# Two chunks of 256 tokens made one stretch of 512: input groups first, then four output tiles

## The chip, the cores and the metric

The kernel runs on one core of a Trainium2 chip. A core has five engines with queues of their own: TensorE (PE, with its weight loads as PEld), VectorE (DVE), ScalarE (ACT), GpSimd (POOL) and SyncE (SP, which here issues DMAs). Each runs its instructions in a fixed order and waits on semaphores. The metric is the time of one execution in device microseconds, as a median of runs.

## The reference

Linear attention with random features over 8 batches, 8 heads, 576 tokens and 64 dimensions, then a feed-forward layer over all 4608 tokens.

```
q_p, k_p = phi(q * scale), phi(k * scale)   # exp(x omega^T - |x|^2/2 - max) / sqrt(m), m = 128
kv  = einsum('bhsm,bhsd->bhmd', k_p, v);  z = sum(k_p, axis=2)
x   = (q_p kv) / (q_p z + 1e-6)             # heads joined: [4608, 512]
h   = x @ w_in                              # [4608, 2048]
out = (h * tanh(softplus(h))) @ w_out       # the function in between is "mish"
```

## The kernel before

**Number format.** A factor of a matmul is split into two f16 parts, a high one and a rest; a product is three matmuls (rest x high, high x rest, high x high). The high part is a cast on ACT (`cast`, L69) or DVE (L71), the rest a subtraction on DVE or POOL (`rest`, L78 and L80). The first tasks and chunk 0 are computed in f32 without the split.

**Attention** comes as 68 items in the order of the batches: a `k_task` for each batch and pair of heads (32), a `q_task` for each tile of 128 tokens (36). An item goes through stages: load; cast (`sk` or `sq`, ACT) and rest (POOL); feature matmuls (`pk` or `pq`, PE, L369); maximum and subtraction (DVE, L390 and L399); exp (ACT, L405); cast (`kp` or `qn`, ACT) and rest (DVE). A k item then has v's scaling (`vf`, ACT, L470, needs the scale `s_v` of the batch), its `pkv` matmuls (L482) and their cast. A q item has a transposing DMA (L517), its `pn` matmuls (L532), the division on DVE, the split into `xs` and a second transposing DMA into `xT` (L562), which the feed-forward layer reads.

**Feed-forward** goes by 18 chunks of 256 tokens. `ff_in(c)` makes 8 groups: each computes two blocks f of 128 hidden units for the chunk, 2 x 12 matmuls with 256 columns moving, into one bank of PSUM (`ph`, two buffers). ACT reads a bank with mish into `h` (L694), and after every two banks a split makes the high part of `g` (ACT, L69) and the rest (DVE, L80). Where a chunk holds tokens of two batches, whose scales differ, mish and split are done in two pieces (`spans`). `ff_out(c)` has two `po` tiles (one bank each) and adds up 16 blocks f with three matmuls of 512 columns each; `o_task` scales a finished tile on ACT and stores it.

**Order.** A clock of turns sets it: `step()` is one turn, in which each task on the agenda that is due runs a stage; what it yields is the number of turns to its next stage. From chunk 2 on, each pass of the loop calls `next` of `ff_in(c)`, a turn, `next` of `ff_out(c - 1)`, a turn: input groups of one chunk alternate with output matmuls of the chunk before, one group of 24 against 12. Items are given at the turns of FIRST (the first 18), and later when their count is under `pace`, which rises by about 4 in a chunk. From an item's start its cast comes 3 turns later, the feature matmuls 6, the exp 8; `pkv` 11; `pn` 12 (13 for q7). A late stage of an item is emitted ahead of the mish and split that the same turn holds, since it is older on the agenda. This order is what the program is built from; the scheduler of the framework then places each engine's instructions by priority and by when it expects them to be able to run. `behind_ff` keeps attention matmuls behind the last feed-forward matmul emitted.

**Start.** Chunk 0 and 1 have code of their own (`ff_in(0)`, `ff_in(1)`, `ff_out0`); the weights are split in between (`w_split`).

Of the kernel before, what the change touches and what calls it, by code (L numbers as in the profile page):

```python
# [30 lines left out]
def tile_kernel(  # L31
# [10 lines left out]
    nc = tc.nc  # L42
# [457 lines left out]
    xT = {}  # L500

    def q_task(nth, t):
        c, off = t * P // CH, t * P % CH
        if c not in xT:
            xT[c] = sb.tile([P, 2, KT, CH], F16, tag="xT", name=f"xT{c}", bufs=3)
        tiles = [[(4 * g + i) * P for i in range(4)] for g in range(2)]
        e = yield from features(qT[t], tiles, f"q{t}", nth, t < QF)
        if t < QF:
            yield from q_first(nth, t, e, off)
            return  # L510
        qn = sb.tile([P, 2, H, M], F16, tag="aq", name=f"qn{t}", bufs=QB)
        cast(by("kp", nth), qn[:, 0], e)
        yield 1
        rest(by("kplo", nth), qn[:, 1], e, qn[:, 0])
        yield 1
        qp = sb.tile([P, 2, H, P], F16, tag="ap", name=f"qp{t}", bufs=2)
        nc.sync.dma_start_transpose(  # L517
            out=qp.rearrange("p a h s -> p (a h) s"), in_=qn.rearrange("p a h m -> p (a h m)")
        )
        yield 2 if t > 9 else 3 if t > QF else 4  # L520
        x = sb.tile([P, H, D], F32, tag="x", name=f"x{t}", bufs=2)
        rd = sb.tile([P, H, 1], F32, tag="rd", name=f"rd{t}")
        pns = []
        with behind_ff():
            for g in range(2):
                pn = ps_a.tile([P, 4, D1], F32, tag="a", name=f"pn{t}_{g}", padded_shape=[P, 4, P])
                for i in range(4):
                    h = 4 * g + i
                    for b, lo, hi in spans(t * P, P):
                        must(HP, "kv", b)  # L530
                        for n, (a, y) in enumerate(((1, 0), (0, 1), (0, 0))):
                            nc.tensor.matmul(  # L532
                                out=pn[lo:hi, i, :], lhsT=qp[:, a, h, lo:hi], rhs=kv[b][:, h, y, :],
                                start=n == 0, stop=n == 2,
                            )
                pns.append(pn)
        yield 1
        for g, pn in enumerate(pns):
            hs = slice(4 * g, 4 * g + 4)

            k_den = TOP * TOP * TOP * KVC
            k_num = TOP * TOP * KVC
            dve.tensor_scalar(
                out=rd[:, hs], in0=pn[:, :, D:D1], scalar1=EPS * k_den, scalar2=k_num / k_den,
                op0=ALU.add, op1=ALU.mult,
            )
            dve.reciprocal(out=rd[:, hs], in_=rd[:, hs])
            xt = dve.tensor_tensor(
                out=x[:, hs, :], in0=pn[:, :, 0:D], in1=rd[:, hs].broadcast_to([P, 4, D]),
                op=ALU.mult,  # L550
            )
        anchors[30 + t] = (xt.ins,)
        yield from x_parts(nth, t, x)

    def x_parts(nth, t, x):
        c, off = t * P // CH, t * P % CH
        xs = sb.tile([P, 2, H * D], F16, tag="xs", name=f"xs{t}", bufs=2)
        xf = x.rearrange("p h d -> p (h d)")
        cast(act if nth < 20 else by("x", nth), xs[:, 0], xf)
        rest(by("xlo", nth), xs[:, 1], xf, xs[:, 0])  # L560
        yield 1
        nc.sync.dma_start_transpose(  # L562
            out=xT[c].rearrange("p a k s -> p (a k) s")[:, :, off:off + P],
            in_=xs.rearrange("p a c -> p (a c)"),
        )
        did("x", c)

    def q_first(nth, t, e, off):

        qp = sb.tile([P, H, P], F32, tag="ap", name=f"qp{t}", bufs=2)  # L570
        for g in range(2):
            hs = slice(4 * g, 4 * g + 4)
            pt = ps_a.tile([P, 4, P], F32, tag="a", name=f"pt{t}_{g}")
            for i in range(4):
                nc.tensor.transpose(out=pt[:, i, :], in_=e[:, 4 * g + i, :], identity=ident)
            cast(act, qp[:, hs, :], pt)
        yield 1
        x = sb.tile([P, H, D], F32, tag="x", name=f"x{t}", bufs=2)
        rd = sb.tile([P, H, 1], F32, tag="rd", name=f"rd{t}")
        for g in range(2):  # L580
            hs = slice(4 * g, 4 * g + 4)
            pn = ps_a.tile([P, 4, D1], F32, tag="a", name=f"pn{t}_{g}", padded_shape=[P, 4, P])
            for i in range(4):
                for b, lo, hi in spans(t * P, P):
                    must(HP, "kvf", b)
                    nc.tensor.matmul(
                        out=pn[lo:hi, i, :], lhsT=qp[:, 4 * g + i, lo:hi], rhs=kvf[b][:, 4 * g + i, :],
                        start=True, stop=True,
                    )
            dve.tensor_single_scalar(out=rd[:, hs], in_=pn[:, :, D:D1], scalar=EPS, op=ALU.add)  # L590
            dve.reciprocal(out=rd[:, hs], in_=rd[:, hs])
            if t * P < CH:
                xt = dve.tensor_tensor(
                    out=x[:, hs, :], in0=pn[:, :, 0:D], in1=rd[:, hs].broadcast_to([P, 4, D]),
                    op=ALU.mult,
                )
                continue
            for b, lo, hi in spans(t * P, P):
                xt = dve.scalar_tensor_tensor(
                    out=x[lo:hi, hs, :], in0=pn[lo:hi, :, 0:D], scalar=vstate[b][2][lo:hi],  # L600
                    in1=rd[lo:hi, hs].broadcast_to([hi - lo, 4, D]), op0=ALU.mult, op1=ALU.mult,
                )
        anchors[30 + t] = (xt.ins,)
        if t * P >= CH:
            yield from x_parts(nth, t, x)
            return
        yield 1
        px = ps_a.tile([P, KT, P], F32, tag="a", name=f"px{t}")
        for i in range(KT):
            nc.tensor.transpose(out=px[:, i, :], in_=x[:, 2 * i:2 * i + 2, :], identity=ident)  # L610
        anchors[40 + t] = (cast(act, xT0()[:, :, off:off + P], px).ins, xt.ins)
        if off == 0:
            spin(2, ident, x[:, 0:4, :].rearrange("p h d -> p (h d)"))
        did("x", 0)

    def xT0():
        return xT[0].rearrange("p a k s -> p (a k s)").bitcast(F32).rearrange("p (k s) -> p k s", k=KT)  # L620

    def g0(gr):
        return gT[0, gr].rearrange("p a f s -> p (a f s)").bitcast(F32).rearrange("p (f s) -> p f s", f=FG)
# [31 lines left out]

    def ff_in(c):

        must(2, "x", c)
        sp = [(b_scales(b) if c else None, lo, hi) for b, lo, hi in spans(c * CH, CH)]
        for gr in range(FT // FG):  # L660
            gT[c, gr] = sb.tile([P, 2, FG, CH], F16, tag="g", name=f"g{c}_{gr}", bufs=GB)
            for q in range(FG // FQ):
# [4 lines left out]
                for j in range(0, FQ, 2):  # L667
                    ph = ps_h.tile([P, 2, CH], F32, tag="h", name=f"ph{c}_{gr}_{q}_{j}")
                    for i in range(2):
# [4 lines left out]
                        for n, (a, y, k) in enumerate(mm):  # L674
                            ff_mm[0] = nc.tensor.matmul(  # L675
                                out=ph[:, i, :], lhsT=wi(a, k, f) if c else wi0(k, f),
                                rhs=xT[c][:, y, k, :] if c else xT0()[:, k, :],
                                start=n == 0, stop=n == len(mm) - 1,
                            )
                    if c == 0:  # L680
# [4 lines left out]
                    else:  # L685
                        later(1, mish, sp, h[:, j:j + 2, :], ph)
                        if j > 0:
                            later(2, g_split, c, gr, q, sp, h)
                    yield

    def mish(sp, h, ph):

# [9 lines left out]
    def g_split(c, gr, q, sp, h):  # L702
        sl = slice(q * FQ, (q + 1) * FQ)
        did("g", c, q)
        g = gT[c, gr]
        for us, lo, hi in sp:
            cast(by_c("g", c), g[:, 0, sl, lo:hi], h[:, :, lo:hi], us[:, 1:2])
            lo_ = rest(dve, g[:, 1, sl, lo:hi], h[:, :, lo:hi], g[:, 0, sl, lo:hi], us[:, 1:2])
        anchors["g"] = (lo_.ins, anchors["h"])

# [40 lines left out]
        nc.sync.dma_start(out=out[row:row + P, :], in_=o)  # L751


    GB, HB, QB = 4, 5, 1
    w_dma = nc.sync

    FIRST = (0, 1, 2, 3, 4, 4, 9, 9, 26, 28, 30, 32, 37, 40, 44, 58, 59, 68)
    WIS = (6, 7, 8, 9, 11, 12, 13, 14)
    W_MAX = (6, 5, 5, 4, 2, 2, 1, 1)
    WOS = (35, 34, 33, 32, 31, 30, 29, 28)  # L760
# [10 lines left out]
    GAP0 = {'load': 1, 'exp': 0, 'kv': 1}  # L771
    GAP = {'load': 3, 'hi': 1, 'lo': 2, 'exp': 1, 'kv': 2}

    ROLE = dict(hi="AA", lo="PP", kp="AA", kplo="DD", v="DD", vlo="PP", kv="AA", x="AD", xlo="PP", h="DD", h0="DD", gm="DD", g="DA", glo="PD")
    NE, CE = 9, 1
    ENG = {"A": act, "D": dve, "P": pool}

    def gap(what, name):
# [7 lines left out]

    def by(role, nth):
        return ENG[ROLE[role][nth >= NE]]

    def by_c(role, c):  # L790
        if c == 0 and role[0] == "h":
            return act
        return ENG[ROLE[role][c >= CE]]

    wmax = []
    for n in (0, 1):
# [94 lines left out]
    load_v(2, nc.sync)  # L891
    load_v(3, act)
    load_w(0)
    load_two("q", qT, 0, "xT", 3)
    for i in range(1, NB):
        load_w(i)
    start(v_task(0))
# [27 lines left out]
        step()  # L925
        step()
    next(fo, None)
    for c in range(2, NCH):
        fi, fo = ff_in(c), ff_out(c - 1)
        for j in range(8):  # L930
            if given[0] < min(pace(c + j / 8), len(items)):
                give()
            next(fi, None)
            step()
            next(fo, None)
            step()
        for gen in (fi, fo):
            next(gen, None)
    while agenda:
        step()  # L940
    for _ in ff_out(NCH - 1):
        step()
    while agenda:
        step()

# [40 lines left out]
```

## Time and profile before

| what | value |
|---|---|
| runs shown | 957.12, 955.04, 954.8 us; median 955.04 us |
| profiled execution | 957.28 us, its span 955.5 us |
| granted TensorE clock, mean | 0.995 |
| PE, ACT, DVE, POOL busy | 97%, 67%, 55%, 26% of the span |
| ph matmuls (L675) | 3392, of which 128 in f32 |
| po matmuls (L719) | 1632 |

The page gives busy time by engine, then slices of the span, DMA queues, the chain of work that ended last, and the costliest groups of instructions by line. In the timeline a row has start, length, engine, line, operation, names (out<-in), shapes and count, and in brackets how long the engine was idle before it and what ended that. In the chain a row has start, length and what was running. In the windows a row has the stretch, its length, busy time and count for PE, PEld, DVE, ACT and POOL, the granted clock, the busy share of the DMA engines and GB/s. A time of a helper's line (L69, L78, L80) belongs to many tiles; the names tell them apart. The mean duration of a matmul in a group (278 and 380 ns) is that of one matmul by itself; in a row of many they overlap, and the distance from start to start is less.

### The profile page before, as it was taken

The numbers are of one execution on the slowest core, as the hardware profiler recorded it, in microseconds if no ns is written. First come the engines' busy times: TensorE is split into PE (matmuls) and PEld (weight loads), VectorE is DVE, ScalarE is ACT, GpSimd is POOL, SyncE is SP. The second block draws the span as 40 slices with busy tenths as digits, with TensorE's granted clock in tenths as the row PEclk, the third lists the DMA queues.
The fourth block names the chain that finished last, engine by engine and source line by source line (L and its number), as shares of the span: only waits on it lengthen the run. The fifth ranks groups of instructions, "written<-read, shape, count | busy, mean of one in ns | idle before, by whom it ended". The sixth has DMA issues, their size and how long they took to land. (4 is left out here: it accounts for less than half of the span.)

```text
span 955.5 us, 19211 instructions
## 1 busy us (share of the span) xinstructions
PE 931.4 (97%) x8125; PEld 665.1 (70%) x8125; DVE 528.2 (55%) x930; ACT 641.1 (67%) x831; POOL 247.6 (26%) x153
## 2 busy tenths in 40 slices
PE   9899987999999999999999999999999999999998
PEld 6786753767777777777777776777777777666663
DVE  3879688584775476655665464654746555111110
ACT  5758885798787777777777675877857766332230
POOL 1313143252162125322433243321442130000000
PEclk9998999999999999999999999999999999999999
DMA  9954414432452247214432245302430233100000
GB/s 288 320 190 155 136 47 100 84 96 71 92 118 62 56 69 165 59 48 85 95 66 72 46 95 113 95 24 70 79 91 23 68 56 84 28 23 12 12 12 34
DMA packets 128214, 82.22 MB, mean 86 GB/s; under 512 B 106432, under 2 KB 106560, under 8 KB 128128
## 3 DMA queue, kind: packets, MB, share of 16 engines
q1 hardware_dynamic: 127392, 79.47, 33.4%
q10 hardware_dynamic: 736, 1.52, 0.6%
q8 instruction: 64, 1.05, 0.4%
q14 instruction: 22, 0.18, 0.1%
HBM read 46.37 MB, written 9.44 MB: 58 GB/s over the span
## 5 line engine op out<-in xcount | busy, mean ns | idle before, releaser
L675 PE MATMUL ph<-xT,w 128*128 128x256 f16 (+1 forms) x3392 | 411.2, 278 | 0.7 <-ACT xT L69 0.7
L719 PE MATMUL po<-wo,g 128*128 128x512 f16 x1632 | 374.3, 380 | 4.1 <-ACT wo L69 2.8
L675 PEld LDWEIGHTS <-w 128*128 128x128 f16 x3264 | 318.5, 98 | 61.8 <-issue 1.6
L719 PEld LDWEIGHTS <-g 128*128 128x128 f16 x1632 | 155.9, 98 | 168.1 <-issue 5.0
L694 ACT ACTIVATE h<-ph,us 128x512 f32<-128x512 f32 (+3 forms) x184 | 101.1, 574 | 201.2 <-PE ph L675 200.2
L80 DVE SCALAR_TENSOR_TENSOR g<-h,us,g 128x1024 f16<-128x1024 f32 (+3 forms) x92 | 104.6, 1150 | 132.2 <-ACT g L69 131.9
L78 POOL TENSOR_TENSOR sq<-fq,sq 64x1024 f16<-64x1024 f32 x31 | 74.4, 2401 | 225.7 <-ACT sq L69 125.0
L78 POOL TENSOR_TENSOR sk<-fk,sk 64x1152 f16<-64x1152 f32 x24 | 62.8, 2618 | 81.2 <-ACT sk L69 53.1
L69 ACT ACTIVATE g<-h,us 128x1024 f16<-128x1024 f32 (+3 forms) x92 | 82.4, 924 | 1.1
L78 POOL TENSOR_TENSOR xs<-x,xs 128x512 f16<-128x512 f32 x34 | 46.8, 1377 | 125.4 <-issue 69.1
L390 DVE TENSOR_REDUCE mxk<-pk 128x4 f32<-128x512 f32 (+1 forms) x96 | 49.6, 549 | 50.7 <-PE pk L369 37.1
L390 DVE TENSOR_REDUCE mxq<-pq 128x4 f32<-128x512 f32 x72 | 46.6, 682 | 51.1 <-PE pq L369 48.4
L694 ACT ACT_TABLE_LOAD x56 | 71.8, 1283 | 1.0
L405 ACT ACT_TABLE_LOAD x52 | 66.7, 1283 | 0.9
L78 DVE TENSOR_TENSOR qn<-eq,qn 128x1024 f16<-128x1024 f32 x31 | 39.4, 1270 | 46.1 <-ACT qn L69 46.1
L78 DVE TENSOR_TENSOR kp<-ek,kp 128x1152 f16<-128x1152 f32 x24 | 38.6, 1610 | 18.6 <-ACT kp L69 18.6
L69 ACT ACTIVATE o<-po,us 128x512 f32<-128x512 f32 (+1 forms) x38 | 25.9, 682 | 30.3 <-PE po L719 30.2
L405 ACT ACTIVATE eq<-eq,lnt 128x1024 f32<-128x1024 f32 x31 | 35.6, 1149 | 9.0 <-DVE eq L399 8.6
L78 POOL TENSOR_TENSOR vb<-vf,vb 128x640 f16<-128x640 f32 x24 | 35.7, 1496 | 19.5 <-DVE vb L71 17.9
L399 DVE TENSOR_TENSOR eq<-pq,mxq 128x512 f32<-128x512 f32 x62 | 39.8, 679 | 0.0
L399 DVE TENSOR_TENSOR ek<-pk,mxk 128x512 f32<-128x512 f32 (+1 forms) x72 | 37.5, 548 | 0.5
L369 PE MATMUL pq<-om,sq 128*128 128x128 f16 x496 | 32.8, 219 | 3.7 <-POOL sq L78 3.7
(119 smaller groups left out, 889.9 us busy)
## 6 DMA issues: line engine op xcount, KB each, us to landing
vf<-in_vL_dram SPq DMA_DIRECT2D x30, 325.0 KB, 3.5
out_dram<-o SPq DMA_DIRECT2D x36, 256.0 KB, 2.1
fq<-in_qT_dram SPq DMA_DIRECT2D x31, 256.0 KB, 3.4
fk<-in_kT_dram SPq DMA_DIRECT2D x24, 256.0 KB, 3.6
raw<-in_w_out_dram SPq DMA_DIRECT2D x5, 1024.0 KB, 6.8
wo<-in_w_in_dram SPq DMA_DIRECT2D x4, 1024.0 KB, 12.3
raw<-in_w_in_dram SPq DMA_DIRECT2D x4, 1024.0 KB, 14.9
wo<-in_w_out_dram SPq DMA_DIRECT2D x3, 1024.0 KB, 7.9
```

Of the source, the lines that this page charges most:

```text
L69: return act.activation(out, in_, AF.Copy, scale=scale)
L78: eng.tensor_tensor(out=out, in0=in_, in1=hi, op=ALU.subtract)
L80: return eng.scalar_tensor_tensor(out=out, in0=in_, scalar=scale, in1=hi, op0=ALU.mult, op1=ALU.subtract)
L369: nc.tensor.matmul(out=pp[:, i, :], lhsT=left[:, o:o + P], rhs=right, start=j == 0, stop=j == len(terms) - 1,)
L390: sub = dve.tensor_reduce(out=mx[:, lo:hi], in_=pp[:, :m, :], axis=AX.X, op=ALU.max, negate=by_act)
L399: sub = dve.tensor_tensor(out=e[:, lo:hi, :], in0=pp[:, :m, :], in1=mx[:, lo:hi].unsqueeze(2).broadcast_to([P, m, M]), op=ALU.subtract,)
L405: last = act.activation(e, e, AF.Exp, bias=lnt)
L675: ff_mm[0] = nc.tensor.matmul(out=ph[:, i, :], lhsT=wi(a, k, f) if c else wi0(k, f), rhs=xT[c][:, y, k, :] if c else xT0()[:, k, :], start ...
L694: anchors["h"] = act.activation(h[:, :, lo:hi], ph[:, :, lo:hi], AF.Mish, scale=us[:, 0:1]).ins
L719: ff_mm[0] = nc.tensor.matmul(out=po[i], lhsT=gT[c, gr][:, a, f % FG, i * P:(i + 1) * P], rhs=wo(y, f), start=f == 0 and (a, y) == parts[0 ...
```

## The change

From chunk 2 on, chunks are taken in pairs of 512 tokens. `pair_in(g)` computes the 16 blocks f one by one, each with 12 matmuls of 512 columns into one bank; `pair_out(g)` follows with four output tiles, one after the other, 16 blocks f each. The two no longer alternate: 16 turns of one, then 16 turns of the other. Mish works on one block of 512 tokens, the split on two blocks. `h` has four buffers instead of five and holds two blocks of 512 tokens; `g` keeps its four buffers of the same size. `xT` holds a pair and has two buffers instead of three; the pair of chunks 0 and 1 shares one buffer. `pair_in` needs four tiles of x where `ff_in` needed two. `ff_out(1)` runs by itself before the first pair. Two entries of FIRST move: item 15 (q7) from turn 58 to 54, item 17 (k2_0) from 68 to 64. `pace` is unchanged and is asked every second turn. The high part of `g` was a cast on ACT for all these chunks before, too.

```diff
+    def pair_in(g):
+        must(4, "x", g)
+        sp = [(b_scales(b), lo, hi) for b, lo, hi in spans(2 * g * CH, 2 * CH)]
+        x = x_two(g)
+        for f in range(FT):
...
+            ph = ps_h.tile([P, 1, 2 * CH], F32, tag="h", name=f"ph{g}_{f}")
+            mm = [(a, y, k) for a, y in ((1, 0), (0, 1), (0, 0)) for k in range(KT)]
+            for n, (a, y, k) in enumerate(mm):
+                ff_mm[0] = nc.tensor.matmul(
+                    out=ph[:, 0, :], lhsT=wi(a, k, f), rhs=x[:, y, k, :],
+                    start=n == 0, stop=n == len(mm) - 1,
+                )
+            later(1, mish, sp, h[:, f % 2:f % 2 + 1, :], ph)
+            if f % 2 == 1:
+                later(2, pair_split, g, f - 1, sp, h)
+            yield
...
+    def pair_out(g):
+        parts = ((1, 0), (0, 1), (0, 0))
+        for i in range(2 * CH // P):
+            po = ps_o.tile([P, DM], F32, tag="o", name=f"po{g}_{i}")
+            for f in range(FT):
+                must(1, "gp", g, f // 2)
+                for a, y in parts:
...
+                if f == FT - 1:
+                    start(o_task(2 * g, i, po), 1)
+                if f % 4 == 3:
+                    yield
...
-    GB, HB, QB = 4, 5, 1
+    GB, HB, QB = 4, 4, 1
-    FIRST = (0, 1, 2, 3, 4, 4, 9, 9, 26, 28, 30, 32, 37, 40, 44, 58, 59, 68)
+    FIRST = (0, 1, 2, 3, 4, 4, 9, 9, 26, 28, 30, 32, 37, 40, 44, 54, 59, 64)
...
-    for c in range(2, NCH):
-        fi, fo = ff_in(c), ff_out(c - 1)
-        for j in range(8):
-            if given[0] < min(pace(c + j / 8), len(items)):
+    def run(gen, c, n):
+        for j in range(n):
+            if j % 2 == 0 and given[0] < min(pace(c + j / 16), len(items)):
                 give()
-            next(fi, None)
+            next(gen, None)
             step()
-            next(fo, None)
-            step()
...
+    run(ff_out(1), 2, 8)
+    for g in range(1, NCH // 2):
+        run(pair_in(g), 2 * g + 0.5, 16)
+        run(pair_out(g), 2 * g + 1.5, 16)
```

More of the change, by code (lines that the diff above doesn't have):

```diff
@@ L502, in q_task @@
     def q_task(nth, t):
-        c, off = t * P // CH, t * P % CH
-        if c not in xT:
-            xT[c] = sb.tile([P, 2, KT, CH], F16, tag="xT", name=f"xT{c}", bufs=3)
+        off = t * P % CH
+        if t // 4 not in xT:
+            xT[t // 4] = sb.tile([P, 4 * KT * CH], F16, tag="xT", name=f"xT{t // 4}", bufs=2)
         tiles = [[(4 * g + i) * P for i in range(4)] for g in range(2)]
@@ L555, in x_parts @@
     def x_parts(nth, t, x):
-        c, off = t * P // CH, t * P % CH
         xs = sb.tile([P, 2, H * D], F16, tag="xs", name=f"xs{t}", bufs=2)
@@ L562, in x_parts @@
         nc.sync.dma_start_transpose(
-            out=xT[c].rearrange("p a k s -> p (a k) s")[:, :, off:off + P],
-            in_=xs.rearrange("p a c -> p (a c)"),
+            out=x_at(t), in_=xs.rearrange("p a c -> p (a c)"),
         )
-        did("x", c)
+        did("x", t // 4)
     def q_first(nth, t, e, off):
@@ L613, in q_first, with x_two, x_at @@
             spin(2, ident, x[:, 0:4, :].rearrange("p h d -> p (h d)"))
-        did("x", 0)
+        did("x0")
     def xT0():
-        return xT[0].rearrange("p a k s -> p (a k s)").bitcast(F32).rearrange("p (k s) -> p k s", k=KT)
+        return xT[0][:, 0:2 * KT * CH].bitcast(F32).rearrange("p (k s) -> p k s", k=KT)
+    def x_two(g):
+        w = xT[g][:, 2 * KT * CH:] if g == 0 else xT[g]
+        return w.rearrange("p (a k s) -> p a k s", a=2, k=KT)
+    def x_at(t):
+        off = t * P % (2 * CH) - (CH if t < 4 else 0)
+        return x_two(t // 4).rearrange("p a k s -> p (a k) s")[:, :, off:off + P]
     def g0(gr):
@@ L656, in ff_in @@
     def ff_in(c):
-        must(2, "x", c)
+        must(2, "x", 0) if c else must(2, "x0")
         sp = [(b_scales(b) if c else None, lo, hi) for b, lo, hi in spans(c * CH, CH)]
@@ L676, in ff_in @@
                                 out=ph[:, i, :], lhsT=wi(a, k, f) if c else wi0(k, f),
-                                rhs=xT[c][:, y, k, :] if c else xT0()[:, k, :],
+                                rhs=x_two(0)[:, y, k, :] if c else xT0()[:, k, :],
                                 start=n == 0, stop=n == len(mm) - 1,
@@ L689, in ff_in, with pair_split @@
                     yield
+    def pair_in(g):
[3 more added lines that the diff above has]
+        for f in range(FT):
+            if f % FQ == 0:
+                gP[g, f // FQ] = sb.tile([P, 2, FQ, 2 * CH], F16, tag="g", name=f"gp{g}_{f}", bufs=GB)
+            if f % 2 == 0:
+                h = sb.tile([P, 2, 2 * CH], F32, tag="ht", name=f"h{g}_{f}", bufs=HB)
+            ph = ps_h.tile([P, 1, 2 * CH], F32, tag="h", name=f"ph{g}_{f}")
[9 more added lines that the diff above has]
+            yield
+    def pair_split(g, f, sp, h):
+        split(sp, gP[g, f // FQ], slice(f % FQ, f % FQ + 2), h)
+        did("gp", g, f // 2)
+    def pair_out(g):
[5 more added lines that the diff above has]
+                for a, y in parts:
+                    ff_mm[0] = nc.tensor.matmul(
+                        out=po, lhsT=gP[g, f // FQ][:, a, f % FQ, i * P:(i + 1) * P],
+                        rhs=wo(y, f), start=f == 0 and (a, y) == parts[0],
+                        stop=f == FT - 1 and (a, y) == parts[-1],
+                    )
+                if f == FT - 1:
+                    start(o_task(2 * g, i, po), 1)
+                if f % 4 == 3:
+                    yield
+    gP = {}
     def mish(sp, h, ph):
@@ L704, in g_split, with split @@
         did("g", c, q)
-        g = gT[c, gr]
+        split(sp, gT[c, gr], sl, h)
+    def split(sp, g, sl, h):
         for us, lo, hi in sp:
-            cast(by_c("g", c), g[:, 0, sl, lo:hi], h[:, :, lo:hi], us[:, 1:2])
+            cast(act, g[:, 0, sl, lo:hi], h[:, :, lo:hi], us[:, 1:2])
             lo_ = rest(dve, g[:, 1, sl, lo:hi], h[:, :, lo:hi], g[:, 0, sl, lo:hi], us[:, 1:2])
@@ L772, in tile_kernel @@
     GAP = {'load': 3, 'hi': 1, 'lo': 2, 'exp': 1, 'kv': 2}
-    ROLE = dict(hi="AA", lo="PP", kp="AA", kplo="DD", v="DD", vlo="PP", kv="AA", x="AD", xlo="PP", h="DD", h0="DD", gm="DD", g="DA", glo="PD")
-    NE, CE = 9, 1
+    ROLE = dict(hi="AA", lo="PP", kp="AA", kplo="DD", v="DD", vlo="PP", kv="AA", x="AD", xlo="PP", h="DD", h0="DD", gm="DD", glo="PD")
+    NE = 9
     ENG = {"A": act, "D": dve, "P": pool}
@@ L788, in by @@
         return ENG[ROLE[role][nth >= NE]]
[L790 to L793, printed above, removed]
     wmax = []
@@ L893, in tile_kernel @@
     load_w(0)
-    load_two("q", qT, 0, "xT", 3)
+    load_two("q", qT, 0, "xT", 2)
     for i in range(1, NB):
@@ L927, in tile_kernel @@
     next(fo, None)
-    for c in range(2, NCH):
-        fi, fo = ff_in(c), ff_out(c - 1)
-        for j in range(8):
-            if given[0] < min(pace(c + j / 8), len(items)):
+    def run(gen, c, n):
+        for j in range(n):
+            if j % 2 == 0 and given[0] < min(pace(c + j / 16), len(items)):
                 give()
-            next(fi, None)
+            next(gen, None)
             step()
-            next(fo, None)
-            step()
[L937 to L942, printed above, removed]
+        next(gen, None)
+    run(ff_out(1), 2, 8)
+    for g in range(1, NCH // 2):
+        run(pair_in(g), 2 * g + 0.5, 16)
+        run(pair_out(g), 2 * g + 1.5, 16)
     while agenda:
```

## The prediction

> **What bounds the kernel now.** I read the page first, then the chain of work that ended last, then the timeline of ACT beside it.
>
> ```profile
> span 955.5 us, 19211 instructions
> PE 931.4 (97%) x8125; PEld 665.1 (70%) x8125; DVE 528.2 (55%) x930; ACT 641.1 (67%) x831; POOL 247.6 (26%) x153
> L675 PE MATMUL ph<-xT,w 128*128 128x256 f16 (+1 forms) x3392 | 411.2, 278 | 0.7 <-ACT xT L69 0.7
> ```
>
> PE is busy 97% of the span, and the input matmuls (L675) alone are 411 us of it. The chain (start, length, what) shows how they alternate with the output matmuls (L719) and the attention's, without a hole:
>
> ```profile
> 624.45 1.00 PE pk L369 x18
> 625.46 2.59 PE po L719 x12
> 628.05 0.96 PE pkv L482 x30
> 629.00 2.62 PE ph L675 x24
> 631.62 2.59 PE po L719 x12
> ...
> 649.22 0.89 PE pq L369 x16
> ...
> 667.59 0.74 PE pn L532 x24
> ...
> 928.31 23.32 PE po L719 x108
> ```
>
> Each piece starts where the last ends; the last row is the closing ff_out, where no input group stands between. So only two things count: what PE's own work takes, and any hole the change opens in it. The holes come from who must answer PE. One window of ACT's timeline in that stretch, and the busy times of the same 12.38 us (PE, PEld, DVE, ACT, POOL):
>
> ```profile
> 624.49 0.84 ACT L694 ACTIVATE h<-ph,us 128x128 f32<-128x128 f32 x2 [3.01 <-PE ph L675]
> 625.54 1.06 ACT L69 ACTIVATE sq<-fq 64x1024 f16<-64x1024 f32 x1 [0.21 <-issue]
> 626.62 1.28 ACT L405 ACT_TABLE_LOAD   x1
> 627.98 1.26 ACT L405 ACTIVATE ek<-ek,lnt 128x1152 f32<-128x1152 f32 x1
> 629.30 1.15 ACT L69 ACTIVATE kp<-ek 128x1152 f16<-128x1152 f32 x1
> 630.47 1.28 ACT L694 ACT_TABLE_LOAD   x1
> 631.77 0.84 ACT L694 ACTIVATE h<-ph,us 128x128 f32<-128x128 f32 x2
> 632.50 1.33 ACT L69 ACTIVATE g<-h,us 128x256 f16<-128x256 f32 x2
> ...
> 651.27 1.28 ACT L405 ACT_TABLE_LOAD   x1
> 652.56 1.15 ACT L405 ACTIVATE eq<-eq,lnt 128x1024 f32<-128x1024 f32 x1
> ...
> 656.31 0.84 ACT L694 ACTIVATE h<-ph,us 128x128 f32<-128x128 f32 x2
> 624.49:636.87 12.38, 12.38 (x124) 9.00 (x122) 6.99 (x11) 8.99 (x12) 3.54 (x2) 1.00 0.06 21
> ```
>
> See the mish (L694): ACT waited 3.01 us for the first. Between the two lies one k task's block: table load, exp, kp, table load back. The two mish end 7.28 us apart (625.33 and 632.61), and PE never notices: a ph buffer is wanted again only after two rounds of ph and po. ACT has 3.4 us of 12.38 free.
>
> **The change, part by part.**
>
> *Columns.* 24 matmuls of 256 columns take 2.62 us, 12 of 512 take 2.59 (the po rows: same form as the new ph). Chunks 2 to 17 hold 8 x 16 = 128 such groups: 128 x 0.03 = 3.8 us less. This is the whole gain on PE; the number of columns is unchanged, and weight loads, which fall by 1536, lie beside matmuls (9.00 of 12.38). Nor does a long run of 512 go at another pace than an alternating one: 23.32/108 = 215.9 ns against 2.59/12 = 215.8.
> The Trainium skill, page TensorE: Matmul & The Clock Gate, section Back-to-back issue gap, says that in a sustained stream of weight loads and matmuls one of 512 columns takes some 131 ns, because neighbours overlap. By it the columns would give 1536 x (218 - 131) ns = 134 us instead of 3.8; the 108 matmuls of the last row are such a stream and contradict it.
>
> *Order.* ff_in and ff_out of neighbouring chunks no longer alternate. For 16 turns PE does only ph groups (2.59 us each, one bank each, two banks), then for 16 turns only po. In the first phase the mish of group n must end before group n+2 starts. Where PE used to give ACT two rounds, it now gives it one group plus the attention matmuls in between.
>
> *ACT's load.* In a k window like the one above it gets two more mish and one more g: 8.99 + 2 x 0.84 + 1.33 = 12.0 us, against 4 x 2.59 + 1.00 + 0.96 = 12.3 us of PE. It just fits, with no room for order. DVE gets one more rest of about g's 1.33 (6.99 + 1.33 = 8.3 of 12.3): hidden. Batch edges (every 576 tokens) cut 7 of 8 pairs, where they cut 6 of 16 chunks; the window above is of a cut chunk, so the price of two mish and two g per group is in it. In the po phase ACT has little to do and needs fewer table loads; that frees time nobody waits for: 0.
>
> *The holes, one per exp in a ph phase.* A task's exp is due 8 turns after it is given. From FIRST and pace I count the exps that fall into the seven ph phases beside attention: 17 of k, 10 of q; three are at turn 0, where no mish is due yet: 15 and 9 are left, four turns apart. Let f0 be the group whose turn holds pk (or pq). Two orders of ACT are possible.
> First, the exp stands before f1's mish. pk ends 1.00 after f0, its exp starts 2.53 later (625.45 to 627.98), f1's mish ends 4.63 after that (632.61): 8.16. PE is through f1, pkv and f2 at 1.00 + 2.59 + 0.96 + 2.59 = 7.14 and waits 1.02. For q: 0.89 + 2.45 + 4.59 = 7.93 against 0.89 + 2.59 + 2.59 + 0.74 = 6.81: 1.12. Sum 15 x 1.02 + 9 x 1.12 = 25.4 us.
> Second, f1's mish goes first, and f2's is late: 1.00 + 2.59 + 0.84, then 5.99 from the table load at 626.62 to 632.61: 10.42, against 9.73 on PE: 0.69; for q 0.89 + 2.59 + 0.84 + 5.88 = 10.20 against 9.40: 0.80. Sum 17.6 us.
> I take the second: ACT's order is by what can run, as the next fence shows with four vf scalings of four tasks in a row. Ends: 0, if the blocks find a gap; and 25.4 + 24 x 1.33 = 57 us, if a g stands in each gap too. Behind a waiting ph stand the attention matmuls of the next turns on PE; their DVE and ACT work moves along with them, so PE doesn't win a hole back.
>
> *Batch starts.* ACT stands in order behind vf, which waits for the scale of v; that was hidden:
>
> ```profile
> 557.81 2.99 ACT L470 ACTIVATE vf<-vf,s_v 128x640 f32<-128x640 f32 x4 [4.79 <-DVE s_v L122]
> ```
>
> Of one such wait in a ph phase a group of 2.59 covers a part: 4.79 - 2.59 = 2.2. I take 2, ends 0 and 6 (three batch starts).
>
> *x earlier.* pair_in needs four x tiles, ff_in needed two. The transposes wait on SP's queue, and xT has two buffers of double size instead of three.
>
> ```profile
> 184.16 0.90 PE L532 MATMUL pn<-kv,qp 128*128 128x65 f16 x24
> 192.55 1.25 SPq L562 DMA_TRANSPOSE xT<-xs  x1
> ...
> 806.99 0.75 PE pn L532 x24
> 812.05 1.34 SPq L562 DMA_TRANSPOSE xT<-xs  x1
> xT<-xs SPq DMA_TRANSPOSE x34, 3.1
> ```
>
> From pn to xT it takes 8.4 + 3.1 = 11.5 us early, 5.1 + 3.1 = 8.2 late. q7, given at 54 instead of 58, has its pn in turn 67; pair_in(1) starts at turn 73, five po groups (13.0 us) later: covered by 1.5. The tightest later is the seventh pair, three groups (7.8 us) after its last pn: short by 0.4. Cost 0, ends 0 and 5 (a q7 late by two turns). q7 and k2_0 also move four turns into the stage that splits w_out; DVE and ACT do that work then instead of later, ends -2 and 4, taken 0. HB 5 to 4: an h now serves two groups and is free after their split, eight groups of room: 0. The g buffers are read before pair_in writes them again: 0.
>
> Sum: -3.8 + 17.6 + 2 = +15.8 us. The profiled run took 957.28 (span 955.5); the runs shown have a median of 955.04, and I put the sum on that: 970.8, forecast 971.
>
> **The rivals.**
> *The cover holds.* If ACT's order puts the exp blocks where a mish isn't next, only the columns are left: 951. For it: 12.0 fits into 12.3, PE's queue stood without holes. Against: a block of 6 us in a stretch that must answer every 2.59. It turns at 3.8/24 = 0.16 us for each exp. Chance 0.20. Between, gain and holes cancel (955): 0.10.
> *ACT becomes the bound, or the clock falls.* With g in the gaps 955 - 4 + 57 + 2 = 1010; half of that 982. Holes can also cost clock:
>
> ```profile
> 161.83 0.59 PE L719 MATMUL po<-wo,g 128*128 128x512 f16 x2 [2.76 <-ACT wo L69]
> 165.00:170.00 5.00, 5.00 (x42) 3.61 (x41) 1.84 (x2) 3.45 (x5) 2.12 (x1) 0.76 0.54 116
> ...
> 576.50 0.92 PE L532 MATMUL pn<-kv,qp 128*128 128x65 f16 x24 [1.83 <-DMA qp<-qn]
> 575.00:580.00 5.00, 3.50 (x38) 2.08 (x39) 2.33 (x7) 3.03 (x3) 1.34 (x1) 1.00 0.92 215
> ```
>
> After the wait of 2.76 (and a shorter one behind it) the granted clock was 0.76 for 5 us: 1.2 us lost. After one of 1.83 it stayed 1.00. With every hole costing that: 24 x 1.2 = 29 us, 1000. My holes are about 0.7, under both. Chance of over 985 by the two: 0.19. The Trainium skill (TensorE: Matmul & The Clock Gate, section A second HAM failure mode: psum-queue depth-cycling) tells of just such a stream, 512 columns cycling through PSUM banks, whose short idles between groups let the clock go up and down. The row at 576.50 shows that one idle of that size does not do it here; no row shows many in a row.
> *A faster 512.* If the new ph groups overlapped so far that a matmul took half its 215.8 ns, 1536 x 0.108 = 166 us would go: 789. The 108 matmuls of the chain's last row speak against it. Chance 0.01.
>
> **How the numbers follow.** Forecast, holes of 8 to 34 us: 0.50, its own range 959 to 985. Faster by over 0.3% (about what this measurement can tell from no change): 0.20 + 0.01; within: 0.10; slower: 0.50 + 0.19. The range leaves out the far parts: 950 (columns alone, and a little) to 992.
>
> **What would show it.** Right: PE waits at the ph line on ACT's mish, some 24 holes of 0.5 to 1.1 us, all in ph phases; po phases closed; ph matmuls 215.8 ns apart; fewer table loads in all; ACT near full in ph phases and half idle in po phases. Wrong: no hole at ph (then 951), a hole at the first ph of pair 1 for xT, or a granted clock under 1.00 after 200 us.

## The result, and the profile after

The changed kernel takes 966.64 us (median of 6 runs, 964.65 to 968.59) against 954.92 for the kernel before on the same chip: 1.0121 times its time, interval 1.01 to 1.0141, so 11.7 us slower. The forecast was 971, the sum of the terms +15.8. The profiled run shown below took 968.59 (span 966.8); the spans differ by 11.3.

The page of the changed kernel, its span, its engines, and from the groups the new input matmuls (L711), the output matmuls of a pair (L731), and the table loads:

```profile
span 966.8 us, 16212 instructions
...
PE 933.5 (97%) x6589; PEld 516.4 (53%) x6589; DVE 519.0 (54%) x962; ACT 600.8 (62%) x889; POOL 231.7 (24%) x153
...
L711 PE MATMUL ph<-xT,w 128*128 128x512 f16 x1536 | 343.6, 380 | 8.3 <-ACT h L746 8.0
L731 PE MATMUL po<-wo,gp 128*128 128x512 f16 x1536 | 345.3, 381 | 3.0 <-DVE gp L80 3.0
...
L746 ACT ACT_TABLE_LOAD x37 | 47.5, 1283 | 0.6
...
L405 ACT ACT_TABLE_LOAD x33 | 42.3, 1283 | 0.6
```

The same two groups of table loads in the page of before:

```profile
L694 ACT ACT_TABLE_LOAD x56 | 71.8, 1283 | 1.0
L405 ACT ACT_TABLE_LOAD x52 | 66.7, 1283 | 0.9
```

ACT shed 38 table loads and 40 us of busy time, and the kernel is still slower: ACT's work in all is not what decides. The column that matters is the last one of L711, idle time of PE just before the group and who ended it. Before, the input matmuls had 0.7 us there in all, in chunk 0, and none from chunk 2 on; now they have 8.3, and 8.0 of it ended when ACT had emptied a ph bank. L731 has 3.0 of its own. PE's waits in the changed kernel (us in total, times, longest) name both:

```profile
PE ph L711 <- ACT h L746: 8.0, 11, 2.6
...
PE po L731 <- DVE gp L80: 3.0, 1, 3.0
```

The pace of the 512-column matmuls is as before. In the chain, the last two phases, an input phase and an output phase without attention:

```profile
880.06 41.44 PE ph L711 x192
921.50 41.45 PE po L731 x192
```

They give 215.8 and 215.9 ns a matmul and follow each other without a gap. Where the attention is done, nothing is lost; the loss lies where its exps stand between ACT's mish. At all eleven waits for mish a table load, an exp and the table load back stand just ahead of the mish, or of a piece of it, that PE waited for. One such place, on ACT's timeline of the changed kernel:

```profile
516.72 0.84 ACT L746 ACTIVATE h<-ph,us 128x256 f32<-128x256 f32 x2 [0.78 <-PE ph L711]
517.45 1.33 ACT L69 ACTIVATE gp<-h,us 128x512 f16<-128x512 f32 x2
518.79 1.28 ACT L405 ACT_TABLE_LOAD   x1
520.09 1.26 ACT L405 ACTIVATE ek<-ek,lnt 128x1152 f32<-128x1152 f32 x1
521.36 1.28 ACT L746 ACT_TABLE_LOAD   x1
522.66 0.84 ACT L746 ACTIVATE h<-ph,us 128x256 f32<-128x256 f32 x2
523.39 1.16 ACT L69 ACTIVATE kp<-ek 128x1152 f16<-128x1152 f32 x1
```

Two mish (L746) stand about 6 us apart, with a g split, two table loads and the exp between them. Compare this with ACT's timeline of before in the prediction: kp used to stand ahead of the second mish and now stands behind it, and the g split took its place. A mish of a pair with tokens of two batches is done in two pieces, and in five of the eleven waits, 5.3 of the 8.0 us, kp or the exp came between the pieces: ahead of the longest wait, the one that ended at 202.12, the pieces start at 200.18 and 201.45 and a kp of 1.15 us stands between them. The same stretch and four others on PE's timeline:

```profile
202.12 4.44 PE L711 MATMUL ph<-xT,w 128*128 128x512 f16 x12 [2.56 <-ACT h L746]
...
214.50 2.75 PE L711 MATMUL ph<-xT,w 128*128 128x512 f16 x12
217.09 2.32 PE L731 MATMUL po<-wo,gp 128*128 128x512 f16 x10
219.25 5.34 PE L711 MATMUL ph<-xT,w 128*128 128x512 f16 x24
...
257.72 7.03 PE L731 MATMUL po<-wo,gp 128*128 128x512 f16 x18 [2.96 <-DVE gp L80]
...
523.54 7.93 PE L711 MATMUL ph<-xT,w 128*128 128x512 f16 x36 [0.50 <-ACT h L746]
...
605.37 10.82 PE L711 MATMUL ph<-xT,w 128*128 128x512 f16 x48 [1.41 <-ACT h L746]
```

Three things are to be read. At 523.54 PE waited 0.50 us for the mish that ended there: the predicted hole. At 217.09 PE does ten matmuls of the pair's *output* in the middle of its input phase: the order of PE's instructions is made when the kernel is built, and it put work that was ready into places where an input group would have had to wait. At 202.12 twelve matmuls take 4.44 us, where the twelve at 214.50 take 2.75, so they ran partly at half speed, and this follows the longest wait at ph. The windows of the changed kernel (window, length, then busy us of PE, PEld, DVE, ACT, POOL, granted clock, DMA share, GB/s) show that clock, and the two kinds of phases at full clock (the first of these two windows starts with 2.6 us of the output phase before):

```profile
200.00:205.00 5.00, 2.88 (x8) 1.11 (x8) 3.14 (x5) 4.17 (x9) 1.40 (x1) 0.73 0.38 114
...
255.00:260.00 5.00, 2.28 (x6) 0.89 (x7) 5.00 (x10) 1.15 (x1) 1.30 (x2) 0.69 0.49 111
260.00:265.00 5.00, 5.00 (x22) 2.06 (x20) 1.34 (x5) 2.31 (x3) 0.38 (x1) 0.62 0.14 53
...
296.60:343.00 46.40, 45.84 (x339) 24.36 (x338) 27.04 (x40) 40.14 (x60) 9.91 (x5) 1.00 0.21 57
353.27:398.30 45.03, 44.76 (x328) 23.31 (x326) 28.73 (x67) 20.03 (x21) 17.10 (x12) 1.00 0.59 117
```

In an input phase ACT is busy 40.1 of 46.4 us, in an output phase 20.0 of 45.0. In the first three windows the clock is short by 0.27, 0.31 and 0.38 of 5 us: 4.8 us. What it cost PE is read from the matmul rows: 4.44 − 2.75 = 1.7 us at 202.12, and at 257.72 eighteen matmuls in 7.03 us, where 18 x 0.216 and 0.16 for the end of the last make 4.05: 3.0 us. Together 4.7: 22 matmuls, 8 of the input and 14 of the output, lay 0.43 us apart instead of 0.216.

The account against before starts with a lead: up to the first output matmuls of chunk 1, where little but FIRST differs, the changed kernel is 2.1 us early (159.74 against 161.83). From there to the end it loses 13.4 us: columns −4.0 (measured below), waits at ph +8.0, the wait at po +3.0, slow clock +4.7, which makes +11.7. The rest is about what each of these twelve waits costs beyond its idle time: the last matmul ahead of it lasts 0.38 us, where the next would start after 0.216, so 12 x 0.16 = 2.0 us. PE's other idle time differs by less than 1 us.

### The profile page after: what moved, and what is told of

It reads as the page before. It is cut to its first block, busy times and chain, and to the rows that moved or that the text cites. A ratio compares the mean times of both kernels' runs of the same rounds, so it can differ in the third digit from the quotient of the medians.

```text
span 966.8 us, 16212 instructions
## 1 busy us (share of the span) xinstructions
PE 933.5 (97%) x6589; PEld 516.4 (53%) x6589; DVE 519.0 (54%) x962; ACT 600.8 (62%) x889; POOL 231.7 (24%) x153
## 4 chain that ended last, share of the span: by engine, by line
PE 72%; ACT 12%; DVE 3%; DMA 3%; issue 1%; POOL 1%; SPq 0%; ACTq 0%; POOLq 0%; DVEq 0%
PE po L731 33%; PE ph L711 26%; DMA qp<-qn 3%; ACT h L746 2%; PE pq L369 2%; PE pn L532 2%; ACT L746 2%; PE pk L369 2%; ACT L405 2%; PE pkv L482 1%; ACT gp L69 1%; PE ph L682 1%; PE po L773 1%; ACT ek L405 1%; PE po L790 1%
## 5 line engine op out<-in xcount | busy, mean ns | idle before, releaser
L711 PE MATMUL ph<-xT,w 128*128 128x512 f16 x1536 | 343.6, 380 | 8.3 <-ACT h L746 8.0
L731 PE MATMUL po<-wo,gp 128*128 128x512 f16 x1536 | 345.3, 381 | 3.0 <-DVE gp L80 3.0
L711 PEld LDWEIGHTS <-w 128*128 128x128 f16 x1536 | 148.9, 98 | 183.0 <-issue 13.5
L731 PEld LDWEIGHTS <-gp 128*128 128x128 f16 x1536 | 148.2, 98 | 173.9 <-issue 3.9
L80 DVE SCALAR_TENSOR_TENSOR gp<-h,us,gp 128x128 f16<-128x128 f32 (+7 forms) x120 | 100.4, 857 | 128.1 <-ACT gp L69 127.5
L746 ACT ACTIVATE h<-ph,us 128x64 f32<-128x64 f32 (+7 forms) x248 | 111.2, 493 | 79.4 <-PE ph L711 73.2
L69 ACT ACTIVATE gp<-h,us 128x128 f16<-128x128 f32 (+7 forms) x120 | 83.9, 749 | 0.3
L69 ACT ACTIVATE sk<-fk 64x1152 f16<-64x1152 f32 x24 | 27.8, 1160 | 43.6 <-PE pq L369 15.0
L682 PE MATMUL ph<-xT,w 128*128 128x256 f16 (+1 forms) x320 | 53.6, 323 | 0.7 <-ACT xT L69 0.7
L69 ACT ACTIVATE sq<-fq 64x1024 f16<-64x1024 f32 x31 | 32.6, 1052 | 33.5 <-issue 30.5
```

Of the source, the lines that this page charges most:

```text
L69: return act.activation(out, in_, AF.Copy, scale=scale)
L80: return eng.scalar_tensor_tensor(out=out, in0=in_, scalar=scale, in1=hi, op0=ALU.mult, op1=ALU.subtract)
L682: ff_mm[0] = nc.tensor.matmul(out=ph[:, i, :], lhsT=wi(a, k, f) if c else wi0(k, f), rhs=x_two(0)[:, y, k, :] if c else xT0()[:, k, :], st ...
L711: ff_mm[0] = nc.tensor.matmul(out=ph[:, 0, :], lhsT=wi(a, k, f), rhs=x[:, y, k, :], start=n == 0, stop=n == len(mm) - 1,)
L731: ff_mm[0] = nc.tensor.matmul(out=po, lhsT=gP[g, f // FQ][:, a, f % FQ, i * P:(i + 1) * P], rhs=wo(y, f), start=f == 0 and (a, y) == parts[0],
L746: anchors["h"] = act.activation(h[:, :, lo:hi], ph[:, :, lo:hi], AF.Mish, scale=us[:, 0:1]).ins
```

## The experiments

Two ideas stood against each other on the main cost: that the exps' place in the input phases makes the holes (the prediction), or that something else that came with the pairs does (the wider matmul, the moved items, the slow clock). Medians in us, ratios to the kernel before measured beside each (954.92 us for the change, 955.32 for e1 to e4, 954.95 for e5 to e8, 955.68 for e9 and e10). The last column counts waits for mish:

| kernel | time | ratio, interval | PE's waits for mish at the input matmuls |
|---|---|---|---|
| the change | 966.64 | 1.0121, 1.01 to 1.0141 | 8.0 in 11 |
| e1, 256 columns | 963.57 | 1.0095, 1.0067 to 1.0123 | 7.6 in 10 |
| e2, exps in output phases | 989.11 | 1.0363, 1.0336 to 1.039 | 2.6 in 1 |
| e3, third ph bank | 954.53 | 1.0005, 0.9986 to 1.0025 | none |
| e4, no output matmuls ahead | 970.28 | 1.0161, 1.0131 to 1.019 | 17.5 in 18 |
| e5, pairs that alternate | 965.89 | 1.0124, 1.0104 to 1.0145 | none |
| e6, before with the new FIRST | 953.16 | 0.9977, 0.9962 to 0.9993 | none |
| e7, e3 with 256 columns | 958.56 | 1.0052, 1.0031 to 1.0073 | none |
| e8, before with the third bank | 960.90 | 1.008, 1.0049 to 1.0111 | none |
| e9, pairs alternate from the third on | 952.53 | 0.9964, 0.995 to 0.9979 | 1.8 in 1 |
| e10, idle output banks lent to ph | 952.25 | 0.9961, 0.9945 to 0.9977 | 2.0 in 2 |

**e1: the width alone.** The changed kernel's order, with each 512-column matmul as two of 256.

```diff
+            for half in (slice(0, CH), slice(CH, 2 * CH)):
...
-                    out=ph[:, 0, :], lhsT=wi(a, k, f), rhs=x[:, y, k, :],
+                    out=ph[:, 0, half], lhsT=wi(a, k, f), rhs=x[:, y, k, half],
```

> The changed kernel with each 512-column input matmul made of two with 256 columns again (same order of work, twice the weight loads). If the wide matmul really saves its 0.03 us per group and PE is the bound, this is 3.8 us slower than the changed kernel: about 970.4. Rival: in the input phases PE waits on ACT anyway and the longer matmuls only eat holes: 966 to 967, with the wait of ph on mish falling by 2 to 3 us from 8.0.

Its median is 3 us under the change's; the two intervals overlap, so that it is faster isn't shown, but the 970.4 expected lies outside its own. Its waits:

```profile
PE ph L712 <- ACT h L747: 7.6, 10, 1.4
...
PE po L732 <- DVE gp L80: 1.8, 1, 1.8
```

The holes are there with the old width too, so the width doesn't make them. The longest fell from 2.6 to 1.4 and that at po from 3.0 to 1.8, and the clock rose to between 0.993 and 0.996 in its runs, from 0.989 to 0.992 in those of the change. The price of the columns can't be read from this kernel; e7 was made for it.

**e2: the exps moved into the output phases.** The items are given so that the exps come due there (`slot[0]` is the turn); v's scale is started 8 turns after a batch's last k item.

```diff
-            if j % 2 == 0 and given[0] < min(pace(c + j / 16), len(items)):
+            if slot[0] in (65, 67) or slot[0] >= 73 and (slot[0] - 73) % 32 in range(8, 24, 2):
...
-                start(v_task(it[1] + 1), V1 if it[1] != 1 else V2)
+                start(v_task(it[1] + 1), V2 if it[1] == 1 else 8 if it[1] else V1)
```

> The changed kernel with the items of pair phases given at such turns that their exps fall into the output phases (one each two turns; v's scale started 8 turns after the last k item instead of 16). If the holes come from exps standing between a group's mish and the group after next, PE's wait at ph for mish goes from 8.0 us to under 2 and the time to about 957. Rival: the holes come from ACT's load in input phases whatever the exps (mish in two pieces, g casts) or the denser items make new waits in the output phases: 963 to 968.

```profile
PE pk L369 <- DVE x L548: 7.7, 3, 3.1
PE pq L369 <- POOL sq L78: 5.7, 3, 3.3
PE pk L369 <- DVE rd L543: 4.3, 3, 2.4
...
PE pn L532 <- DVE x L548: 3.1, 2, 1.6
PE ph L711 <- ACT h L746: 2.6, 1, 2.6
```

Ten of the eleven waits at ph are gone, as the exps' place demands: 6 exps are left in its input phases, of 27 in the change (17 of k and 10 of q, as the prediction counted). The whole is 22 us slower than the change for another reason: items given every second turn instead of every fourth bunch up, and the attention's own chains (feature matmuls, DVE, next feature matmuls) are now waited for, at a clock of 0.98. After 189 us PE's idle time outside the input phases is 22.9 us, against 3.8 in the change. The cause is borne out; as a remedy it fails.

**e3, e8, e7: one more bank.** If the cover of two banks is what is too short, a third closes the holes. The three pools hold two, two and four banks, and it comes from attention's four; e8 prices that loss in the kernel before, where there were no holes. e7 is e3 with the matmuls of e1, without holes that could hide the columns.

```diff
-    ps_h = ctx.enter_context(tc.tile_pool(name="ps_h", bufs=2, space=PSUM))
+    ps_h = ctx.enter_context(tc.tile_pool(name="ps_h", bufs=3, space=PSUM))
...
-    ps_a = ctx.enter_context(tc.tile_pool(name="ps_a", bufs=4, space=PSUM))
+    ps_a = ctx.enter_context(tc.tile_pool(name="ps_a", bufs=3, space=PSUM))
```

> The changed kernel with three PSUM banks for ph and three instead of four for attention. If two banks are what makes a late mish a hole, PE's wait at ph goes from 8.0 us to under 2, the clock drops behind it go too, and the time is 956 to 959. Rival: three banks are too few for attention (a k item takes three for pk alone) and PE waits at pk, pq and pn instead: 966 or more.

> The kernel before with three ph banks and three for attention. It had no wait at ph, so the third bank can give nothing: 955, or 956 to 958 if a bank less for attention costs something at the start. Rival to the reading of the three-bank run: the banks help in themselves, wherever the order: 951 or less.

> Three ph banks and three for attention as in the run before, and each 512-column matmul made of two with 256. With the holes gone, this tells the price of the columns alone: 3.8 us over the run with three banks, 958.3. Rival: the columns save nothing, as the slower time of the changed kernel against its own 256-column form could suggest: 954.5.

The input groups in the page of e3:

```profile
L711 PE MATMUL ph<-xT,w 128*128 128x512 f16 x1536 | 341.8, 379 | 0.0
```

and in that of e7:

```profile
L712 PE MATMUL ph<-xT,w 128*128 128x256 f16 x3072 | 345.8, 273 | 0.0
```

No hole is left in either. e3 is 12 us faster than the change; e8 is 6 us slower than before by the move of the bank alone. Between kernels with equal pools, then, the change is worth 954.53 − 960.90 = −6.4 us once its holes are closed; by the intervals it can be some 3.5 us more or less. Of that the columns are 958.56 − 954.53 = 4.0 us (e7 against e3, some 2.7 us more or less by the intervals; the rows of the prediction, 2.62 against 2.59 us, say 3.8), and the rest is about what e6 finds for FIRST.

**e4: no output matmuls ahead of the last input group.** It undoes what the row at 217.09 showed.

```diff
+        last_in = ff_mm[0].ins
...
+                    with tc.issue_after(last_in):
+                        ff_mm[0] = nc.tensor.matmul(
+                            out=po, lhsT=gP[g, f // FQ][:, a, f % FQ, i * P:(i + 1) * P],
```

> The changed kernel with all output matmuls of a pair kept behind its last input matmul. If output matmuls that PE draws into the input phases fill part of the holes, the wait at ph rises from 8.0 us to about 17 (the sum of the prediction), while the wait of 3.0 us at the first output matmuls of pair 1 and its slow clock go away (about 4): about 971. Rival: their place does not matter, or they only cause the wait in pair 1: 962 to 967.

```profile
PE ph L711 <- ACT h L748: 17.5, 18, 2.6
```

The holes are now 17.5 us; the prediction's term for them was 17.6. It came as 18 waits of 0.16 to 2.56 us instead of 24 of about 0.7, so that the sum met so closely is luck in part. Drawing output matmuls ahead thus hides 9.5 us of holes in the changed kernel. The wait at po on gp is gone with it. And the clock held: the same first wait of pair 1, on PE's timeline of e4, and its window:

```profile
202.74 2.75 PE L711 MATMUL ph<-xT,w 128*128 128x512 f16 x12 [2.56 <-ACT h L748]
```

```profile
200.00:205.00 5.00, 2.44 (x17) 1.14 (x14) 3.21 (x5) 4.79 (x9) 1.40 (x1) 1.00 0.46 122
```

The same 2.56 us of idle at nearly the same time was followed by a granted clock of 0.73 in the change and 1.00 here. So the length of a wait doesn't decide it by itself; what differs is taken up below.

**e6: the moved items alone.** The kernel before, with the two entries of FIRST that the change moves.

```diff
-    FIRST = (0, 1, 2, 3, 4, 4, 9, 9, 26, 28, 30, 32, 37, 40, 44, 58, 59, 68)
+    FIRST = (0, 1, 2, 3, 4, 4, 9, 9, 26, 28, 30, 32, 37, 40, 44, 54, 59, 64)
```

> The kernel before with the two entries of FIRST moved as in the change (q7 at turn 54, k2_0 at 64), nothing else. The prediction took 0 for it: 955 within 1.5. Rival: the denser start costs the splits of w_out and the first output matmuls some us: 957 to 959.

953.16 against 954.95: 1.8 us faster, interval 0.9962 to 0.9993. Not a cause of the slowdown.

**e5 and e9: pairs that alternate.** Input groups of 512 columns keep output matmuls between them: a pair's output runs half a pair behind, two token tiles at a time, so that ACT gets back its two rounds.

```diff
+        for j in range(16):
+            turn(fi)
+            if j == 11:
+                next(fo, None)
+                fo = pair_out(g)
...
+                turn(fo)
```

In e5 the pairs start with the second (chunks 2 and 3 in the old form), in e9 with the third of the changed kernel's pairs (chunks 2 to 5 in the old form), and e9 gives the items more slowly at first, one every 3.3 turns instead of about 2.2. In both, v's scale is started as in e2.

> Pairs as in the change, with 512 columns and two ph banks, but input and output alternate again: from chunk 4 on each input group is followed by a quarter of two output tiles, the outputs half a pair behind (chunks 2 and 3 in the old form; items given somewhat earlier at the start). If it is the order that opens the holes, PE's wait at ph is under 1 us and only the columns are left: 950 to 953. Rival: a mish of 512 columns in one bank is itself too late for two banks: waits at ph of 4 us or more, 958 to 965.

In e5 the input groups have no wait, but the attention does, as its waits and one window show:

```profile
PE pq L369 <- POOL sq L78: 6.7, 3, 2.7
PE pn L532 <- DMA qp<-qn: 5.0, 4, 3.1
PE pk L369 <- DVE x L548: 3.9, 1, 3.9
```

```profile
225.00:250.00 25.00, 18.43 (x182) 12.68 (x181) 20.84 (x38) 23.45 (x25) 14.49 (x9) 0.89 0.64 135
```

PE is busy 18.4 of 25 us there, with ACT at 23.5 and DVE at 20.8; that the items came too densely is the reading that e9 was made for. The time went from one wait to another, and the result is no better than the change. e9 spaces them:

> The alternating form again, but chunks 2 to 5 in the old form and pairs only from the third on, so that items are given about every 3.3 turns at the start instead of every 2.2. In the first alternating run PE never waited at ph for mish, and its loss stood at pk, pq and pn between 226 and 250 us and at 432 us, where items were given densest. If that density was the loss, it is gone: 950 to 953. Rival: pairs need x so early that attention is late wherever they begin: waits at pn, pq or pk of 5 us or more again, 957 or more.

```profile
PE pn L532 <- DMA qp<-qn: 2.0, 4, 0.6
PE ph L711 <- ACT h L749: 1.8, 1, 1.8
```

At 952.53 it beats the kernel before by 0.36% (interval of the ratio 0.995 to 0.9979). As it begins the pairs later and spaces the items too, it doesn't tell which of the two helped.

**e10: the idle banks.** In an input phase the two output banks stand idle but for the output matmuls drawn ahead. Six of a pair's sixteen groups write into them; the attention keeps its four.

```diff
-            ph = ps_h.tile([P, 1, 2 * CH], F32, tag="h", name=f"ph{g}_{f}")
+            lend = f % 4 > 1 and f < 12
+            ph = (ps_o if lend else ps_h).tile(
+                [P, 1, 2 * CH], F32, tag="o" if lend else "h", name=f"ph{g}_{f}"
+            )
```

> The changed kernel in its own order; of the 16 input groups of a pair, groups 2, 3, 6, 7, 10 and 11 write into the two PSUM banks of the output tiles, which stand free in that phase. Attention keeps its four banks. If two banks are the cause, the wait at ph is under 1.5 us and with it the slow clock goes: 951 to 954. Rival: ACT is the bound of these phases, and more banks only move the wait to the first output matmuls: 960 to 966.

```profile
PE ph L714 <- ACT h L749: 2.0, 2, 1.2
```

Holes from 8.0 to 2.0, the wait at po gone, the clock between 0.992 and 0.996: 952.25, some 14 us faster than the change and 0.39% faster than the kernel before (0.9945 to 0.9977). Of these 0.39%, e6 has 0.23% from the moved items without any pairs; what pairs of 512 with closed holes add to that, some 1.5 us, is within the intervals. e10 differs from the change in nothing but where six groups write, so two banks' cover is what the order lacked.

## Why the prediction was right, and where not

- *Direction and mechanism: right.* The order, not the width and not ACT's load as such, costs the time. PE waits at ph on mish, where exps stand in input phases (e2 removes all but one of the waits by moving the exps, e3 all and e10 all but two by adding cover). The output phases closed but for one wait of 3.0 us and two of the attention, 0.6 and 0.3.
- *Columns −3.8: −4.0 measured* (e7 against e3), closer than that measurement can tell. The pace of 512 didn't change: 215.8 ns in 192 matmuls on end, so the rival of a faster 512 is out. The Trainium skill's figure of some 131 ns (TensorE: Matmul & The Clock Gate, section Back-to-back issue gap) is not met by any run here.
- *The holes +17.6: this is the term that was mis-sized; 8.0 us in 11 waits.* Its working assumed that PE does only input groups and attention in an input phase. PE was given output matmuls of the same pair ahead, and they hid 9.5 us; with them kept back (e4) the term measured 17.5. The assumed order of ACT was also off in detail: in six of the eleven waits kp or qn moved behind the late mish and a g split stood in its place. The holes foreseen, some 24 of 0.5 to 1.1 us, were eleven of 0.28 to 2.56.
- *The other side of drawing ahead, not foreseen: +3.0.* In pair 1 the output matmuls reached a gp tile that DVE had not split yet. The timeline of DVE and POOL in the changed kernel, ahead of the wait that ended at 257.72:

```profile
252.78 2.36 POOL L78 TENSOR_TENSOR sk<-fk,sk 64x1152 f16<-64x1152 f32 x1 [10.23 <-ACT sk L69]
...
252.96 2.47 DVE L71 CAST xs<-x 128x512 f16<-128x512 f32 x1
...
255.95 1.71 DVE L80 SCALAR_TENSOR_TENSOR gp<-h,us,gp 128x896 f16<-128x896 f32 x1
...
260.95 0.43 DVE L71 CAST xs<-x 128x512 f16<-128x512 f32 x1
```

  The split came late, behind a cast that took 2.47 us where the same cast takes 0.43 at 260.95. The trace goes some way to say why. POOL's subtraction had started 0.18 us before the cast and ended at 255.14, and the cast ended 0.28 us after it, at 255.43. Of the 27 casts of this tile on DVE in this trace, the 20 that overlap no POOL instruction take 0.42 to 0.43 us, and so does one that POOL's instruction began 0.18 us after; the six that start while a POOL instruction runs take 0.99 to 2.47, and each ends 0.28 us after it. So the cast behaves as if it waited for POOL; no run took POOL's work away to test it.
- *The clock: taken as 0, cost 4.7.* A granted clock under 1.00 after 200 us was among the prediction's own signs of being wrong, and it came (0.73, 0.69, 0.62). The rival's rate of 1.2 us for every hole fell too: ten of the eleven ph waits, up to 1.41 us, left no matmul slow; the clock fell after the waits of 2.56 and 2.96 only, and after an equal 2.56 in e4 it did not. The Trainium skill (TensorE: Matmul & The Clock Gate, section A second HAM failure mode: psum-queue depth-cycling) lets many short idles between groups do this. The 18 waits of e4 don't bear it out: from 168 to 945 us its granted clock was 1.00. The traces show what set the two equal waits apart. In each trace the clock's falls and rises lie whole multiples of 3.41 us apart (202.32, 205.74, 256.94, 263.76 in the change). Windows cut on this grid, first of the change, then of e4:

```profile
198.91:202.32 3.41, 0.84 (x22) 0.65 (x19) 1.24 (x2) 3.40 (x6) 1.40 (x1) 1.00 0.30 77
202.32:205.74 3.42, 3.42 (x9) 1.22 (x8) 2.23 (x4) 1.87 (x4) 0.00 (x0) 0.50 0.34 102
```

```profile
198.50:201.91 3.41, 1.68 (x34) 1.23 (x33) 0.50 (x1) 3.38 (x4) 1.66 (x2) 1.00 0.30 77
201.91:205.33 3.42, 2.59 (x13) 1.16 (x13) 2.97 (x4) 2.89 (x7) 0.42 (x1) 1.00 0.37 102
```

  In the change the whole wait fell into one interval, PE was busy 0.84 of its 3.41 us, and the next was run at 0.50; in e4 the grid cut the wait in two, PE was busy 1.68 and 2.59, and the clock held. So it is in all twelve traces from 190 us on: of the intervals at full clock, the ten with at most 1.32 us of busy PE were followed by one at 0.50, the others, with 1.58 and more, by none. (Earlier there is an exception: in the kernel before, the interval at 75.22 had 1.78 us and was followed by 0.50.) This is read from traces; no run moved a wait on the grid to test it.
- *Batch starts +2: no wait of their own at the vf work was seen.* The first wait of pair 1 was for ACT and not for xT, so *x earlier* at 0 stood. *FIRST at 0: −1.8 alone* (e6), inside its ends.

So +15.8 was forecast from −3.8, 17.6 and 2. Measured were 11.7 more, in which −4.0, 8.0, 3.0 and 4.7, the ends of the waits (2.0) and the lead of FIRST (−2.1) stand. The total lay nearer than the terms, and that is luck: a hole term twice too large stood against costs that weren't in the sum. What stays open is what sets where the grid of the clock lies in a run, and so which wait will meet it badly.

## What to carry to other kernels

Work that alternates with other work gives the engine that empties its buffers twice the time; before pulling the two apart, count how long the first engine goes on before it wants a buffer back (here, with two banks, one group of 2.59 us) and set that against the longest block that the other does in between (here some 6 us). If it doesn't fit, look for buffers that the new order itself leaves idle (e10) before taking them from a neighbour (e3 and e8: 6 us). And when holes are summed from rows, ask what independent work could be drawn into them, and what that work will then be waiting for.

## What the runs showed of the hardware that was not expected

- Twice the columns in a matmul save little: 4.0 us in 1536 by e7 against e3 (some 2.7 us more or less), 2.6 ns for each pair of 256 joined to one of 512; the rows, 2.62 us for 24 against 2.59 for 12, say 2.5.
- The same idle of PE, 2.56 us, was followed by a granted clock of 0.73 in one kernel and of 1.00 in another; ten idles of 0.28 to 1.41 us left it at 1.00. From 190 us on, over twelve traces, the clock went to 0.50 after just those intervals of a 3.41 us grid in which PE was busy for 1.32 us or less.
- A cast of 128x512 from f32 to f16 on DVE took 2.47 us beside a POOL subtraction, and 0.43 us 8 us later without one. All six casts of this kind that started while a POOL instruction ran ended 0.28 us after it.
